# Token order of q, k, v and alpha in a fused gated linear attention and MLP kernel

## The chip, the cores and the metric

The kernel runs on one core of one Trainium2 chip. The metric is the device time of one launch in microseconds, lower is better; a kernel's time is the median of several executions. A separate execution is recorded by the hardware profiler; its span is counted from the first to the last instruction.

The names in the profile: PE is TensorE's matmuls and PEld its weight loads, DVE is VectorE, ACT ScalarE, POOL GpSimd, SP SyncE. SyncE issues nearly all transfers, in program order. A name with a q (SPq) is an engine's instruction queue.

## What is computed

Four batches, eight heads, 768 tokens, head width 48. A recurrent attention with a per-token, per-channel gate `alpha` gives `y`, which is joined over heads to rows of 384 and goes through a layer norm, two matrix products and a residual:

```python
for t in range(S):
    state = alpha[:, :, t, :, None] * state + np.einsum('bhd,bhe->bhde', k[:, :, t], v[:, :, t])
    y[:, :, t] = np.einsum('bhd,bhde->bhe', q[:, :, t], state)
...
xn = (x - mu) / np.sqrt(var + 1e-06) * g_ln
ch = np.maximum(xn @ w_ch1, 0.0) @ w_ch2
return (x + ch)
```

The weights `w_ch1` (384 x 1536) and `w_ch2` (1536 x 384) are double precision; everything else is 32 bits. In memory q, k, v and alpha lie as batch, token, head, width, so one token of one batch is a row of 384 numbers, 1,536 bytes.

## The kernel before

**Tiling.** The tokens are cut into six chunks of 128, one token per partition. `attention(c, b)` (lines 280 to 463) does chunk `c` of batch `b`: ln of alpha (L289), a prefix sum over tokens as a matmul with a triangle, exp of it (L299, L300), scaling of k and q (L302, L304), transposes (L320), scores, masking (L346, L351), the state update `ups` (L367, L376 to L382), the output `yps` (L392, L408), the layer norm and a transposed, scaled copy `xT` (L453, L456, L460) for the MLP. Chunk 0 is done whole (`whole`); in chunks 1 to 5 the 128 tokens are two halves of 64, so that every matmul of the attention covers one quarter, 64 by 64, of the array, and matmuls on different quarters run side by side.

**Pairs of batches.** For chunks 1 to 5 the prefix sums (`sums()`, L471) and the scores (`scores()`, L487) are done for an even and an odd batch together, so that the two use different quarters. In `sums()` the even batch's sum of partition half `h` is written to half `1 - h`: its two halves come out exchanged against alpha's. To match, q, k and v of even batches are loaded with the two halves exchanged: tokens 64 to 127 on partitions 0 to 63. In `attention`, `odd` is 1 for even batches of chunks 1 to 5 (and 0 for odd batches and chunk 0); where the order of tokens counts, the half is `s ^ odd`: state update, gate, and state in the output product. The output rows come out exchanged, and `send` puts them right.

**The second copy of v.** For tokens of half `s` the output product needs v on the partitions on which the scores lie, which is the other half for some heads. `vx`, a second load of half of v's columns with halves placed otherwise, serves these (L163, L164).

**Loads.** `loads("a")`, `loads("k")`, `loads("q")` and `loads_of_v()` yield after each step. Chunk 0 is loaded batch by batch; chunks 1 and 2 two batches at a time (384 KB); chunks 3 to 5 again batch by batch, the odd one first. A load in natural order is one issue (L139, v: L157). A load with the even batch exchanged is a pair of issues, one per partition half, with addresses from `of_pair` (L143, v: L155). `of_pair` gives for half `h` of the partitions the rows of two batches: with `cols` absent, the even batch's half `1 - h` and the odd batch's half `h`.

**Order.** Each unit of work is a generator, and the string `ORDER` names which one takes its next step; every engine runs its instructions in the order in which they were emitted. `0`, `1`, `2` and `3` are the loads of alpha, k, q and v, `4` the sums, `5` the scores, small letters `attention`, `A` to `L` the weight pieces (`take_weights`: load at L207, then the rounding from double to single precision at L219 to L229, in three staging buffers), `Y` and `Z` the first MLP product of chunk 0 (L514), `M` and `V` the later MLP (L626, L803). SyncE's queue also carries, in that order, the gate's way through memory (`row`, L309, then `gate`, L357), the attention's rows (`kept`, L430; read back as `ob`, L497) and the outputs (`send`, L502, L505).

Of the kernel before, what the change touches and what calls it, by code (L numbers as in the profile page):

```python
# [48 lines left out]
def kernel(  # L49
# [36 lines left out]
    nc = tc.nc  # L86

    B, S, H, D = q.shape
    DM = H * D
    DF = w_ch1.shape[1]  # L90
    P = 128
    NCB = S // P
    NP = H // 2
    R = 64 + D
# [15 lines left out]
    HS = P // 2  # L110
    halves = [slice(HS * s, HS * s + HS) for s in range(2)]
    raws = {}

    def of_pair(src, c, m, h, cols=None):

        a = src[2 * m:2 * m + 2, c * P:(c + 1) * P].rearrange("b t h d -> b t (h d)")
        (sb, _), (st, _), _ = a.ap
        if cols is None:
            first, step, n = (1 - h) * HS * st, sb + (2 * h - 1) * HS * st, DM
        else:  # L120
            first, step, n = h * (HS * st + cols), sb + (1 - 2 * h) * (HS * st + cols), cols
        return bass.AP(a.tensor, a.offset + first, [[st, HS], [step, 2], [1, n]])

    def loads(n):

        src = {"a": alpha, "k": k, "q": q}[n]
        lone = None
        for c in range(NCB):
            for m in range(B // 2):
                if c < 3:  # L130
                    t = raw.tile([P, 2, 2, NP, D], FP32, name=f"r{n}", tag="in", bufs=6)
                elif lone is None:
                    t = lone = raw.tile([P, 2, 2, NP, D], FP32, name=f"r{n}", tag="in", bufs=6)
                step = 2 if 0 < c < 3 else 1
                for i in ((0, 1) if c == 0 else (0,) if step == 2 else (1, 0)):
                    bs = slice(2 * m + i, 2 * m + i + step)
                    to = t[:, i:i + step].rearrange("t b i p d -> t b (i p d)")
                    if n == "a" or c == 0 or (step == 1 and i == 1):
                        nc.sync.dma_start(  # L139
                            to, src[bs, c * P:(c + 1) * P].rearrange("b t h d -> t b (h d)"))  # L140
                    else:
                        for h in range(2):
                            nc.sync.dma_start(to[halves[h]], of_pair(src, c, m, h)[:, i:i + step])  # L143
                    raws.update({(n, c, 2 * m + j): t[:, j] for j in range(i, i + step)})
                    yield

    def loads_of_v():
        for c in range(NCB):
            for m in range(B // 2):
                bs, rows = slice(2 * m, 2 * m + 2), slice(c * P, (c + 1) * P)  # L150
                vn = raw.tile([P, 2, 2, NP, D], FP32, name="vn", tag="vn")
                to = vn.rearrange("t b i p d -> t b (i p d)")
                if c:
                    for h in range(2):
                        nc.sync.dma_start(to[halves[h]], of_pair(v, c, m, h))  # L155
                else:
                    nc.sync.dma_start(to, v[bs, rows].rearrange("b t h d -> t b (h d)"))  # L157
                raws.update({("v", c, 2 * m + i): vn[:, i] for i in range(2)})
                yield
                if c:  # L160

                    vx = raw.tile([P, 2, NP, D], FP32, name="vx", tag="vx")
                    for h in range(2):  # L163
                        nc.sync.dma_start(vx[halves[h]].rearrange("t b p d -> t b (p d)"),  # L164
                                          of_pair(v, c, m, h, NP * D))
                    raws.update({("x", c, 2 * m + i): vx[:, i] for i in range(2)})
                    yield
# [100 lines left out]
    def qk_of(c, b):  # L268
        return qks[b if c == 0 else b ^ 1 if c == 1 else (b ^ 1) % 3]
# [10 lines left out]
    def attention(c, b):  # L280


        whole, last = c == 0, c + 1 == NCB
        odd = 0 if whole else 1 - b % 2
# [23 lines left out]
        gate = work.tile([P, 2, NP], FP32, name="gate", tag="gate", bufs=B)  # L308
# [7 lines left out]
        qT = work.tile([R, NP, 2, HS], FP32, name="qT", tag="sum", bufs=11)  # L316
# [14 lines left out]
        if whole:  # L331
            aps = [ps.tile([P, NP, 2, HS], FP32, name=f"aps{i}", tag="bank", bufs=8)
                   for i in range(2)]
            for p in range(NP):
                for i in range(2):
                    rs = slice(64 * i, 64 * i + D)
# [7 lines left out]
        if whole:  # L344
            for i in range(2):
                nc.vector.copy_predicated(  # L346
                    out=at[:, :, i].rearrange("k p s t -> k p (s t)"),
                    data=aps[i].rearrange("k p s t -> k p (s t)"),
                    mask=mask.unsqueeze(1).broadcast_to([P, NP, P]))
        else:  # L350
            nc.vector.copy_predicated(  # L351
                out=at.rearrange("k p s t -> k (p s) t"),
# [10 lines left out]
        for p in range(NP):  # L363
            for s, up in enumerate(ups):
                for i, h in enumerate(heads):
                    ts = slice(0, P) if whole else halves[s ^ odd]
                    nc.tensor.matmul(up[h, p], qk_of(c, b)[ts, 1, p, i, :h.stop - h.start],  # L367
                                     vn[ts, i, p], start=True, stop=True)
        yield

        now, nxt = sts[b][(c + 1) % 2], sts[b][c % 2]
        mid = None if whole else work.tile([R, NP, D], FP32, name="mid", tag="mid", bufs=3)
        for s, up in enumerate(ups):
            by = gate[:R, s ^ odd].unsqueeze(2).broadcast_to([R, NP, D])
            if whole:
                nc.vector.tensor_mul(nxt, up, by)  # L376
                yield
                continue
            old, new = ((now, mid), (mid, nxt))[s]
            nc.vector.tensor_add(new, up, old)  # L380
            yield
            nc.gpsimd.tensor_mul(new, new, by)  # L382
            yield
# [5 lines left out]
        for p in range(NP):  # L389
            for i in range(2 if whole else 0):  # L390
                for s in range(2):
                    nc.tensor.matmul(yps[0][halves[s], i, p], at[:, p, i, s], vn[:, i, p],  # L392
                                     start=True, stop=True)
            for n in range(0 if whole else 8):

                if odd:
                    inner, s, i = n // 4, n // 2 % 2, n % 2
                    r = i
                else:
                    i, s, r = n // 4, n // 2 % 2, n % 2  # L400
                    inner = r != i
                if inner:
                    of, by = at[halves[r], p, s], (vn[halves[r], i, p] if s == r else
                                                   raws["x", c, b][halves[r], p])
                else:
                    rs = slice(64 * i, 64 * i + D)
                    of, by = qT[rs, p, s], (now, mid)[s ^ odd][rs, p]
                nc.tensor.matmul(yps[r][halves[s], i, p], of, by, start=not (odd and inner),  # L408
                                 stop=bool(inner or not odd), skip_group_check=bool(odd))
        yield  # L410
# [87 lines left out]
                yield  # L498

    def send(c, b, cols=slice(0, DM)):  # L500
        if c == 0 or b % 2:
            nc.sync.dma_start(out[b, c * P:(c + 1) * P, cols], ob_of[c, b][:, cols])  # L502
            return
        for h in range(2):
            nc.sync.dma_start(out[b, c * P + HS * (1 - h):][:HS, cols], ob_of[c, b][halves[h], cols])  # L505

    def hidden(h, j):

# [11 lines left out]
    ops_of, ob_of = {}, {}  # L520

    def project(c, b, js):
        if js[0] == 0:
            ops_of[b] = ps.tile([P, DM], FP32, name="ops", tag="bank", bufs=8)
        for j in js:
            nc.tensor.matmul(ops_of[b], hT_of[c][:, j, b], w2[:, j],  # L526
                             start=(j == 0), stop=(j == NJ - 1))
        yield
        if js[-1] == NJ - 1:
            nc.vector.tensor_add(ob_of[c, b], ops_of.pop(b), ob_of[c, b])  # L530
            send(c, b)
            yield
# [86 lines left out]
    def product(c, n):  # L619
# [47 lines left out]
        elif n == 6:  # L667
            sub(o(1))
            late(o(1), e)
            late(o(1), f)  # L670
            send(c, 0)
        elif n == 14:
            copy(out=g, in_=acc)
# [203 lines left out]

    turns = {"YZ"[h]: first_of_chunk_0(h) for h in range(2)}
    turns |= {"012"[i]: loads("akq"[i]) for i in range(3)} | {"3": loads_of_v()}
    turns |= {"PQ"[h]: second_of_chunk_0(h) for h in range(2)}  # L880
    turns |= {"4": sums(), "5": scores()}
    turns |= {chr(ord("a") + n): attention(n // B, n % B) for n in range(NCB * B)}
    turns |= {chr(ord("A") + i): take_weights(i) for i in range(len(pieces))}
    turns |= {"M": mlp(), "V": hidden_products(NCB - 1), "S": combine_first(), "W": combine_weights(), "R": relus(),
# [34 lines left out]
```

## Time and profile before

| what | value |
|---|---|
| median of 3 runs | 434.1 us (433.73 to 434.27) |
| profiled execution, its own time | 432.86 us |
| its span | 431.0 us |
| TensorE clock granted | 1.000 |
| DMA, mean over the span | 105 GB/s, 45.36 MB |

The time of an execution is a little more than its span. In the views that follow, a row of the chain is start, length, what; a row of a timeline is start, duration, engine, line, operation, written tile <- read tiles, count, and in brackets the idle time ahead of it with what ended it. That releaser is inferred: where the engine named had long been done, it was something else, often a transfer. Rows of stretches give the busy time of each engine with the count of its instructions, the granted clock, the mean busy share of the 16 DMA engines and the bytes moved.

### The profile page before, as it was taken

What the parts mean: (1) busy time and instruction counts of PE and PEld (TensorE: products, weight loads), DVE (VectorE), ACT (ScalarE), POOL (GpSimd) and SP (SyncE); (2) the same over time, 40 slices, a digit from 0 to 9 for tenths busy, and PEclk for the clock granted to TensorE, in tenths of its full rate; (3) what the DMA queues carried; (4) which work ended last, traced back from release to release, by engine and by line L of the source; (5) the groups of instructions that cost most, each with busy time, mean ns of one, the idle gap of its engine ahead of it and who ended that gap; (6) DMA issues with size and microseconds to landing.
All of it is one profiled execution on the core that took longest, in us unless ns stands there. A gap on an engine that the chain in (4) does not pass through costs nothing.

```text
span 431.0 us, 11712 instructions
## 1 busy us (share of the span) xinstructions
PE 420.9 (98%) x4760; PEld 373.1 (87%) x4760; DVE 331.2 (77%) x634; ACT 205.9 (48%) x539; POOL 152.2 (35%) x171
## 2 busy tenths in 40 slices
PE   7998999999999999999999999999999999999996
PEld 6887888856778889998889988898998899999996
DVE  4997999899997978886758768657595669675972
ACT  6684556662762567723773353663518442311200
POOL 3020103010027381236652243671154551637313
PEclk9999999999999999999999999999999999999999
DMA  7789788796363343323314034301014000002201
GB/s 256 199 233 256 221 203 186 226 281 177 101 184 107 93 132 84 104 59 91 86 53 123 20 102 104 74 2 40 2 57 128 2 0 3 0 20 63 66 18 55
DMA packets 52717, 45.36 MB, mean 105 GB/s; under 512 B 24076, under 2 KB 48780, under 8 KB 52664
## 3 DMA queue, kind: packets, MB, share of 16 engines
q1 hardware_dynamic: 52264, 44.62, 37.6%
q8 instruction: 37, 0.61, 0.6%
q14 instruction: 16, 0.13, 0.1%
q10 hardware_dynamic: 400, 0.00, 0.1%
HBM read 35.08 MB, written 9.53 MB: 103 GB/s over the span
## 4 chain that ended last, share of the span: by engine, by line
PE 89%; DMA 5%; DVE 2%; ACT 1%; SPq 1%; issue 1%; DVEq 0%
PE ops L626 30%; PE hps L803 30%; PE ops L526 7%; PE hps L514 6%; PE yps L408 4%; PE tps L320 3%; PE aps L487 2%; DMA ra<-in_alpha_dram 2%; PE ups L367 2%; PE xps L453 2%; DMA ws<-in_moe_w_ch_dram 2%; DMA vn<-in_v_dram 1%; PE lps L471 1%; DVE w L221 0%; DVE ws L227 0%
## 5 line engine op out<-in xcount | busy, mean ns | idle before, releaser
L642 POOL TENSOR_TENSOR ob<-ob,u 128x192 f32<-128x192 f32 x40 | 26.6, 676 | 70.5 <-DVE ob L639 53.2
L803 PE MATMUL hps<-sum,w 128*128 128x256 f32 x192 | 47.7, 380 | 0.0
L382 POOL TENSOR_TENSOR mid<-mid,gate 112x192 f32<-112x192 f32 x20 | 13.5, 679 | 87.9 <-DVE mid L380 48.0
L626 PE MATMUL ops<-w,hT 128*128 128x192 f32 x224 | 40.5, 327 | 0.0
L803 PEld LDWEIGHTS hps<-sum,w 128*128 128x128 f32 x192 | 35.8, 190 | 4.6
L626 PEld LDWEIGHTS ops<-w,hT 128*128 128x128 f32 x224 | 37.0, 190 | 0.5
L854 ACT ACTIVATE hT<-hT 128x512 f32<-128x512 f32 x48 | 28.2, 630 | 16.1 <-POOL hT L825 6.7
L803 PE MATMUL hps<-xT,w 128*128 128x256 f32 x136 | 35.1, 382 | 0.0
L514 PE MATMUL hps<-xT,w 128*128 128x256 f32 x144 | 33.0, 383 | 1.4 <-DVE w L229 1.4
L526 PE MATMUL ops<-w,hT 128*128 128x384 f32 x96 | 32.0, 488 | 0.0
L514 PEld LDWEIGHTS hps<-xT,w 128*128 128x128 f32 x144 | 26.6, 190 | 5.2 <-issue 1.5
L626 PE MATMUL ops<-ws,sum 128*128 128x192 f32 x160 | 28.6, 327 | 0.0
L803 PEld LDWEIGHTS hps<-xT,w 128*128 128x128 f32 x136 | 25.3, 190 | 3.3 <-DVE hT L835 0.2
L526 PEld LDWEIGHTS ops<-w,hT 128*128 128x128 f32 x96 | 17.7, 190 | 11.6 <-DVE w L229 0.4
L626 PEld LDWEIGHTS ops<-ws,sum 128*128 128x128 f32 x160 | 26.1, 190 | 0.1
L636 DVE TENSOR_TENSOR ob<-ops,ob 128x192 f32<-128x192 f32 x50 | 17.0, 352 | 10.9 <-PE ops L626 5.7
L327 ACT COPY qT<-tps 112x512 f32<-112x512 f32 x24 | 13.9, 584 | 23.1 <-PE tps L320 23.0
L626 PE MATMUL ops<-ws,hT 128*128 128x192 f32 x128 | 23.9, 328 | 0.9 <-issue 0.9
L320 PE MATMUL tps<-consts,qk 128*112 128x128 f32 x176 | 23.3, 274 | 0.5 <-DVE qk L304 0.5
L822 POOL TENSOR_TENSOR hT<-hT,u 128x512 f32<-128x512 f32 x8 | 10.8, 1356 | 33.7 <-DVE u L821 33.7
L320 PEld LDWEIGHTS tps<-consts,qk 128*112 128x112 f32 x176 | 19.9, 134 | 3.2 <-issue 1.1
L626 PEld LDWEIGHTS ops<-ws,hT 128*128 128x128 f32 x128 | 21.1, 190 | 1.4 <-issue 1.2
(240 smaller groups left out, 1129.1 us busy)
## 6 DMA issues: line engine op xcount, KB each, us to landing
ws<-in_moe_w_ch_dram SPq DMA_DIRECT2D x12, 768.0 KB
kept<-x SPq DMA_DIRECT2D x24, 192.0 KB
ob<-kept SPq DMA_DIRECT2D x24, 192.0 KB
vn<-in_v_dram SPq DMA_DIRECT2D x20, 192.0 KB
rq<-in_q_dram SPq DMA_DIRECT2D x18, 192.0 KB
rk<-in_k_dram SPq DMA_DIRECT2D x18, 192.0 KB
ra<-in_alpha_dram SPq DMA_DIRECT2D x16, 192.0 KB
out_dram<-ob SPq DMA_DIRECT2D x30, 96.0 KB
```

What stands on the lines that cost most here:

```text
L320: nc.tensor.transpose(tps[:, p], qk_of(c, b)[:, i, p].rearrange("p a b -> p (a b)")[:, :R], ident)
L327: nc.scalar.copy(out=qT, in_=tv)
L382: nc.gpsimd.tensor_mul(new, new, by)
L408: nc.tensor.matmul(yps[r][halves[s], i, p], of, by, start=not (odd and inner), stop=bool(inner or not odd), skip_group_check=bool(odd))
L514: nc.tensor.matmul(hps, w1[:, j // 2, f, j % 2 * P:][:, :P], xT_of[0][:, f, bs], start=(f == 0), stop=(f == NF - 1))
L526: nc.tensor.matmul(ops_of[b], hT_of[c][:, j, b], w2[:, j], start=(j == 0), stop=(j == NJ - 1))
L626: nc.tensor.matmul(acc, lhs[:, j], rhs[:, j], start=(j == 0), stop=(j == NT - 1))
L636: nc.vector.tensor_add(x, acc, x)
L642: getattr(nc.gpsimd, f"tensor_{op}")(x, x, y)
L803: nc.tensor.matmul(acc[:, i], w, b, start=True, stop=True)
L822: add_late(c4, c4, u2)
L854: nc.scalar.activation(out=x, in_=x, func=AFT.Relu)
```

## The change

q, k and v are loaded in natural token order everywhere. Even batches of chunks 1 to 5 have alpha loaded with the halves exchanged instead, so that the sums, which exchange them again, come out in natural order. `odd` no longer enters the choice of halves; the second copy of v gets other addresses to match; the outputs of even batches leave in one issue. `ORDER`, `sums()` and `scores()` stay as they are, and so does every matmul's shape and count.

```diff
         (sb, _), (st, _), _ = a.ap
+        first = (1 - h) * HS * st
         if cols is None:
-            first, step, n = (1 - h) * HS * st, sb + (2 * h - 1) * HS * st, DM
+            step, n = sb + (2 * h - 1) * HS * st, DM
         else:
-            first, step, n = h * (HS * st + cols), sb + (1 - 2 * h) * (HS * st + cols), cols
+            first, step, n = first + h * cols, sb + (1 - 2 * h) * cols, cols
...
-                    if n == "a" or c == 0 or (step == 1 and i == 1):
+                    if n != "a" or c == 0 or (step == 1 and i == 1):
                         nc.sync.dma_start(
                             to, src[bs, c * P:(c + 1) * P].rearrange("b t h d -> t b (h d)"))
                     else:
...
-                if c:
-                    for h in range(2):
-                        nc.sync.dma_start(to[halves[h]], of_pair(v, c, m, h))
-                else:
-                    nc.sync.dma_start(to, v[bs, rows].rearrange("b t h d -> t b (h d)"))
+                nc.sync.dma_start(to, v[bs, rows].rearrange("b t h d -> t b (h d)"))
...
-                    ts = slice(0, P) if whole else halves[s ^ odd]
+                    ts = slice(0, P) if whole else halves[s]
...
-            by = gate[:R, s ^ odd].unsqueeze(2).broadcast_to([R, NP, D])
+            by = gate[:R, s].unsqueeze(2).broadcast_to([R, NP, D])
...
-                    of, by = qT[rs, p, s], (now, mid)[s ^ odd][rs, p]
+                    of, by = qT[rs, p, s], (now, mid)[s][rs, p]
...
     def send(c, b, cols=slice(0, DM)):
-        if c == 0 or b % 2:
-            nc.sync.dma_start(out[b, c * P:(c + 1) * P, cols], ob_of[c, b][:, cols])
-            return
-        for h in range(2):
-            nc.sync.dma_start(out[b, c * P + HS * (1 - h):][:HS, cols], ob_of[c, b][halves[h], cols])
+        nc.sync.dma_start(out[b, c * P:(c + 1) * P, cols], ob_of[c, b][:, cols])
```

In numbers of issues: k and q each lose 10 (one for each of the four two-batch loads of chunks 1 and 2, one for each of the six loads of an even batch in chunks 3 to 5), v loses 10, the outputs lose 10, alpha gains 10.

## The prediction

> **What bounds the kernel now.** I read the page first, then the chain of waits in order of time, the waits of TensorE, and last the issues of the SyncE queue. From the page:
>
> ```profile
> span 431.0 us, 11712 instructions
> PE 420.9 (98%) x4760; PEld 373.1 (87%) x4760; DVE 331.2 (77%) x634; ACT 205.9 (48%) x539; POOL 152.2 (35%) x171
> PE   7998999999999999999999999999999999999996
> PE 89%; DMA 5%; DVE 2%; ACT 1%; SPq 1%; issue 1%; DVEq 0%
> ```
>
> TensorE is busy for 98% of the span and is 89% of the chain. The DMA share of the chain, 5%, must then sit where the row of slices has its 7 and 8: at the start. The chain in order of time (start, length, what) says where:
>
> ```profile
> 8.22 6.39 DMA vn<-in_v_dram
> 14.62 1.73 DMA gate<-row
> 16.35 4.23 DMA ra<-in_alpha_dram
> 20.61 0.52 ACT la L289
> ...
> 29.03 0.61 SPq L143
> ...
> 30.35 6.85 DMA ws<-in_moe_w_ch_dram
> 37.22 0.58 DVE w L219
> ...
> 41.71 0.97 DVE w L229
> 42.81 9.31 PE hps L514 x42
> ...
> 427.43 0.36 DVE ob L636
> ```
>
> Until 42.81 us the chain is loads and what they release: v of chunk 0, alpha of chunk 1, then the second weight piece (ws at 30.35, called B here), which VectorE rounds from 37.22 to 42.68. From 42.81 on it is TensorE to the end. The change removes no matmul, so it can gain by bringing the 42.81 forward, and in the last microseconds after TensorE. TensorE's waits after 30 us:
>
> ```profile
> PE hps L514 <- DVE w L229: 1.4, 1, 1.4
> ```
>
> TensorE had finished what comes before at 42.81 - 1.4 = 41.4 and stood for B.
>
> **Whole loads against halved ones.** Before, a two-batch load of v, k or q behind chunk 0 is a pair of issues, each into 64 partitions. Busy time by stretch (TensorE, weight loads, VectorE, ScalarE, GpSimd, clock, DMA share, GB/s):
>
> ```profile
> 7.00:11.00 4.00, 3.53 (x22) 2.43 (x22) 2.83 (x6) 3.51 (x9) 0.00 (x0) 1.00 1.07 372
> 69.00:71.00 2.00, 2.00 (x108) 1.74 (x107) 1.93 (x3) 1.01 (x3) 1.86 (x2) 1.00 1.07 229
> 43.00:97.00 54.00, 53.98 (x728) 42.51 (x727) 50.68 (x84) 33.11 (x80) 7.01 (x11) 1.00 0.83 223
> ```
>
> In the first stretch whole loads are under way, in the second halved ones; the DMA engines are full in both. 384 KB are 393,216 bytes: 1.06 us at 372 GB/s, 1.72 us at 229. So a load made whole saves **0.66 us** of transfer, and one cut in two (alpha) costs as much.
>
> The row stands first; the Trainium skill, SBUF — State Buffer, section "Door 1: The DMA port swizzle", says that 64 partitions reach 8 of the 16 DMA ports, measures 196 GB/s there against 328 at 1 MiB, and says that two transfers to the two halves do not add up. By those figures an estimate is 0.8 us for each such load in place of the row's value; alpha, now the only one cut, would pay 0.3 us more over its two early loads, which speaks for the slower rival below.
>
> Issues of the SyncE queue (start, duration):
>
> ```profile
> 8.22 0.43 SPq L157 DMA_DIRECT2D vn<-in_v_dram  x1
> 8.75 0.26 SPq L309 DMA_DIRECT2D row<-eq  x1
> 9.06 0.33 SPq L139 DMA_DIRECT2D rq<-in_q_dram  x1
> 9.44 1.43 SPq L143 DMA_DIRECT2D rk<-in_k_dram  x2
> 10.98 0.37 SPq L309 DMA_DIRECT2D row<-more  x1
> 11.40 0.34 SPq L357 DMA_DIRECT2D gate<-row  x1
> 12.61 0.22 SPq L309 DMA_DIRECT2D row<-more  x1
> ...
> 14.99 1.26 SPq L143 DMA_DIRECT2D rq<-in_q_dram  x2
> 16.35 1.30 SPq L139 DMA_DIRECT2D ra<-in_alpha_dram  x1
> ...
> 24.20 1.90 SPq L155 DMA_DIRECT2D vn<-in_v_dram  x2
> 26.14 1.25 SPq L143 DMA_DIRECT2D rk<-in_k_dram  x2
> ...
> 28.50 0.35 SPq L430 DMA_DIRECT2D kept<-x  x1
> 28.94 1.35 SPq L143 DMA_DIRECT2D rq<-in_q_dram  x2
> ```
>
> A whole 384 KB load is issued in 0.43 us, a pair in 1.25 to 1.90. Ahead of B five pairs become singles: 7.19 us of issuing become about 5 x 0.45 = 2.25, and 5 x 0.66 = 3.3 us of transfer go. Two alpha loads (chunk 1) become pairs: +0.8 us of issuing and +0.66 us of transfer each.
>
> **What of this is on the path, step by step.**
>
> Step 1, B's issue. SyncE waits at 28.50 for x (kept). Behind it stands only the q pair, then B. 1.35 becomes 0.45: B goes out at 29.45 in place of 30.35, **-0.9**.
>
> Step 2, B's flight, 6.85 us in a line behind v, k and q. Only q shorter: -0.66; all three: -2.0. B lands at 29.45 + 4.9 to 6.2 = 34.3 to 35.6, not at 37.20.
>
> Step 3, VectorE must be free for it. Its rows (and the wait in brackets), with TensorE's weight load of the same time:
>
> ```profile
> 29.12 0.66 PEld L367 LDWEIGHTS ups<-vn,qk 64*64 64x64 f32 x32 [0.71 <-DVE ws L227]
> 33.73 0.56 DVE L304 TENSOR_TENSOR qk<-rq,more 128x384 f32<-128x384 f32 x1 [0.65 <-DMA rq<-in_q_dram]
> 35.07 1.01 DVE L456 TENSOR_TENSOR xT<-xps,small 128x384 f32<-128x384 f32 x2
> ```
>
> It is done with L456 at 36.08, after 0.65 us of standing for q. q is issued 0.9 us shorter and moved 0.66 us faster, so that wait goes: free at 35.43. The later of steps 2 and 3 is about 35.5, so rounding starts **1.7** us earlier and B is ready at 41.0.
>
> Step 4, TensorE must be there by then. The 0.71 us before L367 is put down to L227, which writes ws and nothing that this matmul reads; I take v's pair (24.20, 1.90 us) for the late one. Whole, it is issued 1.4 us shorter: the stall goes, and TensorE arrives at 41.4 - 0.7 = 40.7. L514 then starts near 41.1, **-1.7**. If only step 1 counts it is -0.9; if VectorE's work ahead of L456 moves too, -2.4.
>
> Step 5, alpha of chunk 1, which was on the chain. The gate load at 14.62 reads no v, yet v's landing releases it: it is the eighth issue behind v (8.75, 9.06, two at 9.44, 10.98, 11.40, 12.61, 14.62), so I read that eight are in flight at most. With k a single, the eighth is q: the gate goes near 12.9, q at about 14.65. q takes 0.45, alpha's halves 0.63 each (half of 1.25) or, at worst, 1.30 each: done at 16.4 to 17.7, against 17.65. Adding the 2.93 us that it lands after its issue, and 0.66: 20.0 to 21.3, against 20.58. v's own landing is pushed 0.66 by the first alpha pair, which stands ahead of it, and relieved as much by k behind it, whose halves shared the engines with it. I take 0 for this step, with -0.6 to +0.7.
>
> Step 6, what becomes of the gain later. VectorE is busy for 50.68 of 54 us from 43 to 97, but its chain starts with B, so it moves along. Alpha has no room at one place, chunk 3 (issues; ln; the chain's row of the sums):
>
> ```profile
> 75.81 0.86 SPq L139 DMA_DIRECT2D ra<-in_alpha_dram  x2
> ...
> L289 ACT ACTIVATE la<-ra x2: 526/527/528, 79.9 to 80.7; 128x384 f32<-128x384 f32 x2
> ...
> 81.23 0.90 PE lps L471 x6
> ```
>
> The second ln ends as the sums start, and with them everything behind on TensorE. The even batch's load becomes two issues (+0.6) and moves slower (192 KB: 0.53 to 0.86, +0.33). The queue ahead is lighter, so I hand back **+0.4**, between 0 and 0.9.
>
> Step 7, the tail:
>
> ```profile
> 426.52 1.11 SPq L505 DMA_DIRECT2D out_dram<-ob  x2
> 427.72 1.02 SPq L502 DMA_DIRECT2D out_dram<-ob  x2
> ```
>
> The second issue at L502 starts near 428.3, behind the pair and its neighbour, though its add ended at 427.43 + 0.36 = 427.79. With one issue fewer ahead it goes at once: **-0.45**.
>
> Costed at nothing: the other 8 output pairs (TensorE's matmuls cover them), and the row order of the even batches' update matmuls, which no row of before shows apart. A matmul there takes about 0.22 us:
>
> ```profile
> L367 PE MATMUL ups<-vn,qk x112: 199/218/253, 14.7 to 30.8; 64*64 64x48 f32 x32, 64*48 64x48 f32 x32, 128*64 128x48 f32 x24, 128*48 128x48 f32 x24
> ```
>
> One fill more or less at each border of the 10 even updates is at most ±2.2 us; inside an update the tiles still alternate, so I take 0.
>
> Sum: -1.7 + 0.4 - 0.45 = -1.75 us. The profiled execution took 432.86 with its span of 431.0; the median is 1.24 above it, and I carry the difference over: 434.1 - 1.75 = 432.3. Its own range is 431.2 (-2.4, nothing handed back) to 433.3 (step 1 and the tail alone, 0.55 of it lost).
>
> **Rivals.**
>
> *Everything moves.* v of chunk 0 lands about 1 us earlier, since k behind it is whole; then alpha, VectorE and TensorE all gain that microsecond, and nothing is handed back: -1.75 - 1.0 - 0.4, **430.9**. For it: v takes 6.39 us, far over 1.06. Against: the alpha pair ahead of it.
>
> *The gain is eaten.* VectorE's 94% from 43 to 97 or a load leaves TensorE waiting until the 1.7 are gone; only the tail is left: **433.6**. Against: TensorE waits nowhere there now.
>
> *Slower: cut alpha becomes the late load.* Place: ln of chunk 1's second pair, at 20.61. v at +0.66 holds q to 15.3; with 0.45 for q and 1.30 for alpha's first half the second goes out at 17.05. If the line before it is as full as v's was (6.39 us from issue to landing), it lands at 23.4; I take 22.9, ln late by 2.3. VectorE's room is 37.22 - 35.43 = 1.8, so it decides from an ln at 22.4. At +2.3 VectorE is done with L456 at 36.08 + 2.3 - 0.65 = 37.7, B is ready 0.5 late, and chunk 3 adds 0.9 with no room: 0.5 + 0.9 - 0.45 = +0.95, **435.1**. Against: q and k give back issue time right ahead of it.
>
> *It does not do what it says.* The words name other column tiles for the scores, but the scores are not in the diff and no matmul is added or dropped; this case has the times above and no chance of its own.
>
> **How the numbers follow.** Forecast 0.55, everything moves 0.13, eaten 0.18, slower 0.14. What can be told from no change is 0.2%, 0.87 us. Faster: 0.55 + 0.13 = 0.68; same: 0.18; slower: 0.14. The range runs from 430.6, below "everything moves", to 434.6, which leaves out most of the slower case and holds the eaten one and much of the update matmuls' bound.
>
> **What would show it.** Right: L514's first wait for L229 under 0.6 us and its start near 41.1; B issued before 29.6 and landed by 35.7; no stall before the first L367 of chunk 1; the gate near 12.9; one issue at L502 following 427.79 at once. Step 5 is wrong if ln (20.61) starts after 21.3; step 6 if the sums of chunk 3 follow their ln later than TensorE could run them, or by more than 0.9 us. The forecast is wrong if L514 starts after 42, or if TensorE shows new waits of over 1 us between 43 and 427.

## The result, and the profile after

| comparison (the kernel before on the same chip) | before, median | changed, median | ratio and its 95% interval |
|---|---|---|---|
| first, 7 and 7 runs | 433.69 us | 430.42 us | 0.9933 [0.9911, 0.9956] |
| again, 23 and 12 runs | 432.35 us | 430.50 us | 0.9963 [0.9936, 0.9990] |

The change is faster, by 3.3 us in the first comparison and 1.9 us in the second; 432.3 us and -1.75 us had been forecast. The direction held. The range of 430.6 to 434.6 had been written for a kernel before at 434.1 us, and a ratio of 0.9933 makes 431.2 of that, inside the range; 430.42 itself, beside a kernel before of 433.69, lies 0.2 us below it. Where the granted clock of each run is on record, the 77 of 93 runs of the kernel before with 0.998 or more have a median of 432.4 us and the 18 of 19 such runs of the changed kernel 430.4, a difference of 2.0 us; runs with a lower clock took longer. Most terms of the sum did not hold, and most of this part is about that. The page of the changed kernel, first profile:

```profile
span 428.4 us, 11650 instructions
PE 420.9 (98%) x4760; PEld 372.9 (87%) x4760; DVE 330.7 (77%) x634; ACT 205.9 (48%) x539; POOL 153.2 (36%) x171
PE 87%; DMA 6%; DVE 3%; ACT 1%; issue 1%; SPq 0%; POOL 0%; DVEq 0%; ACTq 0%
```

Engine work is what it was; the 62 instructions fewer are semaphores and DMA issues. The chain of waits of the changed kernel (start, length, what):

```profile
14.85 5.75 DMA ra<-in_alpha_dram
...
20.68 0.52 ACT la L286
...
29.52 7.14 DMA ws<-in_moe_w_ch_dram
...
36.68 0.57 DVE w L216
...
41.09 0.97 DVE w L226
...
42.20 9.31 PE hps L507 x42
...
79.38 6.25 DMA ws<-in_moe_w_ch_dram
...
87.80 0.66 DVE at L348
...
88.50 8.01 PE ops L519 x24
...
425.60 0.36 DVE ob L629
```

It is the old chain with new line numbers: alpha, then B, then TensorE. L507 (L514 before) starts at 42.20, not near 41.1, although B was issued at 29.52 as foreseen. The SyncE queue (start, duration, issue) shows what alpha did:

```profile
13.29 0.32 SPq L354 DMA_DIRECT2D gate<-row  x1
13.75 0.40 SPq L140 DMA_DIRECT2D rq<-in_q_dram  x1
14.20 1.25 SPq L144 DMA_DIRECT2D ra<-in_alpha_dram  x2
```

In these first profiles alpha of chunk 1 went out 2 us earlier than before (14.20 against 16.35), and its ln started at the same time (20.68 against 20.61). In the second ones, h1 and h2 below, it went out at the same time (14.84 against 14.73), and its ln started 1.5 us later (20.90 against 19.43). Two profiles of each kernel, cut at the start on B and at the last add of the output, say where the time went:

| us | before, 1st | before, 2nd | changed, 1st | changed, 2nd | difference of the means |
|---|---|---|---|---|---|
| first layer on B starts | 42.81 | 42.60 | 42.20 | 42.97 | -0.12 |
| from there to the start of the last add | 384.62 | 383.80 | 383.40 | 382.90 | -1.06 |
| from there to the end of the span | 3.57 | 3.60 | 2.80 | 2.83 | -0.77 |
| span | 431.0 | 430.0 | 428.4 | 428.7 | -1.95 |

So the start, on which the forecast had put -1.7, gave about nothing. The tail gave 0.77. The middle, for which +0.4 was forecast, gave 1.06. Three more traces below have the same loads as one of the two kernels: e1 and h3 as the changed one, h4 as the kernel before. With them the start gives -0.5 us (42.48 in the mean of four, 42.96 in the mean of three) and the middle -0.7; each start spreads over 0.8 to 0.9 us within one kernel.

### The profile page after: what moved, and what is told of

It reads as the page before. It is cut to its first block, busy times and chain, and to the rows that moved or that the text cites. A ratio compares the mean times of both kernels' runs of the same rounds, so it can differ in the third digit from the quotient of the medians.

```text
span 428.4 us, 11650 instructions
## 1 busy us (share of the span) xinstructions
PE 420.9 (98%) x4760; PEld 372.9 (87%) x4760; DVE 330.7 (77%) x634; ACT 205.9 (48%) x539; POOL 153.2 (36%) x171
## 4 chain that ended last, share of the span: by engine, by line
PE 87%; DMA 6%; DVE 3%; ACT 1%; issue 1%; SPq 0%; POOL 0%; DVEq 0%; ACTq 0%
PE ops L619 31%; PE hps L796 30%; PE hps L507 6%; PE ops L519 6%; PE yps L405 4%; DMA ws<-in_moe_w_ch_dram 3%; PE tps L317 3%; DMA ra<-in_alpha_dram 2%; PE ups L364 2%; PE aps L484 2%; PE xps L450 2%; PE lps L468 1%; DMA rq<-in_q_dram 1%; DVE w L218 1%; DVE at L343 1%
## 5 line engine op out<-in xcount | busy, mean ns | idle before, releaser
L619 PE MATMUL ops<-w,hT 128*128 128x192 f32 x224 | 40.7, 327 | 0.1
L847 ACT ACTIVATE hT<-hT 128x512 f32<-128x512 f32 x48 | 28.2, 630 | 16.4 <-POOL hT L818 7.0
L507 PE MATMUL hps<-xT,w 128*128 128x256 f32 x144 | 33.0, 383 | 0.6 <-DVE w L226 0.6
L519 PE MATMUL ops<-w,hT 128*128 128x384 f32 x96 | 32.3, 489 | 0.3 <-DVE at L348 0.3
L507 PEld LDWEIGHTS hps<-xT,w 128*128 128x128 f32 x144 | 26.6, 190 | 4.4 <-issue 0.7
L619 PE MATMUL ops<-ws,sum 128*128 128x192 f32 x160 | 28.6, 327 | 0.0
L519 PEld LDWEIGHTS ops<-w,hT 128*128 128x128 f32 x96 | 17.7, 190 | 12.2 <-DVE at L348 0.9
L619 PE MATMUL ops<-more,sum 128*128 128x192 f32 x120 | 22.0, 326 | 0.0
## 6 DMA issues: line engine op xcount, KB each, us to landing
vn<-in_v_dram SPq DMA_DIRECT2D x12, 384.0 KB, 4.7
```

Source lines behind the costliest of these rows:

```text
L507: nc.tensor.matmul(hps, w1[:, j // 2, f, j % 2 * P:][:, :P], xT_of[0][:, f, bs], start=(f == 0), stop=(f == NF - 1))
L519: nc.tensor.matmul(ops_of[b], hT_of[c][:, j, b], w2[:, j], start=(j == 0), stop=(j == NJ - 1))
L619: nc.tensor.matmul(acc, lhs[:, j], rhs[:, j], start=(j == 0), stop=(j == NT - 1))
L847: nc.scalar.activation(out=x, in_=x, func=AFT.Relu)
```

## The experiments

All kernels but h1, h2 and h4 are the changed kernel with one edit; their medians stand against its 430.45 (the 19 runs of both comparisons).

**Undoing one part at a time.** Three kernels put back one of the halved parts each, and a fourth leaves alpha whole.

e1: the outputs of even batches leave in two issues again.

```diff
-        nc.sync.dma_start(out[b, c * P:(c + 1) * P, cols], ob_of[c, b][:, cols])
+        if c == 0 or b % 2:
+            nc.sync.dma_start(out[b, c * P:(c + 1) * P, cols], ob_of[c, b][:, cols])
+            return
+        for h in range(2):
+            nc.sync.dma_start(out[b, c * P + HS * h:][:HS, cols], ob_of[c, b][halves[h], cols])
```

> The changed kernel, with the outputs of even batches of chunks 1 to 5 sent in two issues again, as before the change. Theory A (the time hangs on when the chain of loads lets TensorE start the first MLP product, L507 at 42.20 us in the changed kernel, and on the last issues after TensorE): only the tail comes back, +0.45 us, a time of about 430.9 and a ratio to the kernel before of 0.9943; L507 stays at 42.2. Theory B (the time follows the number of halved transfers): 10 pairs more, each hidden by matmuls, but half as fast; no place of its own, +0 to +0.5.

e2: v of chunks 1 to 5 in two halves, in natural order.

```diff
-                nc.sync.dma_start(to, v[bs, rows].rearrange("b t h d -> t b (h d)"))
+                vr = v[bs, rows].rearrange("b t h d -> t b (h d)")
+                for h in halves if c else [slice(0, P)]:
+                    nc.sync.dma_start(to[h], vr[h])
```

> The changed kernel, with v of chunks 1 to 5 loaded in natural order but in two issues of 64 partitions each. Theory A: v lands later (about 29 us in place of 27.8) but TensorE waits for a bank until 30.02 anyway, so +0 to +0.3 us, about 430.5, ratio 0.994. Theory B: ten loads at +0.66 us of transfer each, those of chunk 1 and 2 seen: +1 us or more, 431.4 or above.

e3: the same for k and q.

```diff
-                        nc.sync.dma_start(
-                            to, src[bs, c * P:(c + 1) * P].rearrange("b t h d -> t b (h d)"))
+                        rows = src[bs, c * P:(c + 1) * P].rearrange("b t h d -> t b (h d)")
+                        cut = n != "a" and c and not (step == 1 and i == 1)
+                        for h in halves if cut else [slice(0, P)]:
+                            nc.sync.dma_start(to[h], rows[h])
```

> The changed kernel, with k and q of chunks 1 to 5 loaded in natural order but in two issues where the kernel before had two. Theory A: the second weight piece is issued behind one q pair, 0.9 us later (30.4 in place of 29.52), and moves in a longer line; L507 starts at 42.8 to 43.2 in place of 42.20 and the time is +0.6 to +1.0 us, about 431.2, ratio 0.996. Theory B: like v's pairs, +1 us or more.

e4: alpha whole and not exchanged. The exchange is left out, so the gates of even batches belong to the other half of the tokens.

```diff
-                    if n != "a" or c == 0 or (step == 1 and i == 1):
+                    if True:
```

> The changed kernel, with alpha loaded whole, in one issue. It then leaves out the exchange of halves for even batches, so their gates belong to the other half's tokens. Theory A1 (alpha's halves are what delays it): alpha of chunk 1 lands about 1 us before its 20.6, L286 of the second pair starts by 19.7, L507 by 41.3, time -0.9 us, about 429.5, ratio 0.991. Theory A2 (one of the 16 DMA engines is late by 1 to 2 us because a 16 KB piece of program code comes through it at that moment, and holds back alpha and later the weight piece): alpha lands at 20 or later all the same, L507 stays within 0.4 us of 42.2, ratio 0.9925 to 0.994.

| kernel | median, us | ratio to before | first layer on B | last add to end |
|---|---|---|---|---|
| e1, outputs cut | 430.63 | 0.9943 [0.9922, 0.9965] | 42.56 | 3.54 |
| e2, v cut | 431.38 | 0.9968 [0.9946, 0.9990] | 43.17 | 2.90 |
| e3, k and q cut | 433.16 | 1.0005 [0.9982, 1.0028] | 44.03 | 3.05 |
| e4, alpha whole | 428.67 | 0.9906 [0.9886, 0.9927] | 40.49 | 2.96 |

e1 gives back the tail: 3.54 us behind the last add, as before the change. Its median, 0.2 us up, is too near to show the 0.7. e2 and e3 show that the part on the loads was no illusion: whole v is worth 0.9 us of the median (0.3 to 1.7 when the runs are resampled, 95%), whole k and q 2.7 (1.2 to 3.6). Four of e3's twelve runs had a granted clock of 0.996 and took 433.2 us or more; the other eight have a median of 432.3, 1.9 up. e4 shows who takes it back: alpha, cut in halves, costs 1.8 us (1.3 to 2.5). At the start the signs are the same: against the changed kernel's mean of 42.59, cut v is +0.6, cut k and q +1.4, whole alpha -2.1. These are single traces, and 0.6 is within the spread of one kernel; but what v, k and q bring there, 2.0, is about what alpha eats.

**Which alpha.** g1 loads alpha of chunk 1 alone whole, and takes its sums unexchanged; nothing is left out.

```diff
-                    if n != "a" or c == 0 or (step == 1 and i == 1):
+                    if n != "a" or c < 2 or (step == 1 and i == 1):
...
-                        nc.tensor.matmul(lps[halves[h ^ i ^ 1], :DM], tri[halves[h], halves[h]],
+                        nc.tensor.matmul(lps[halves[h if c == 1 else h ^ i ^ 1], :DM], tri[halves[h], halves[h]],
```

> The changed kernel, but chunk 1 has alpha whole and in natural order, and its sums write the natural half for both batches (two matmuls on the same quarter instead of four quarters at once). If halved alpha of chunk 1 alone is what the change pays at the start: ln of the second pair at 18.2 as with alpha whole everywhere, L507 at 40.5 to 41.0 (0.3 us at most for the slower sums), and the time 1.2 to 1.7 us under the changed kernel, about 428.9, ratio 0.990. If halved alpha in chunks 2 to 5 is what cost there: L507 stays near 42.2 and the time near 430.3.

428.61 us, 0.9900 [0.9857, 0.9942]: all of e4's gain, from two loads of one chunk. It beats both kernels. Its chain, where B leaves at 28.64:

```profile
28.64 6.28 DMA ws<-in_moe_w_ch_dram
...
34.94 0.57 DVE w L216
...
39.15 0.97 DVE w L226
...
40.25 5.85 PE hps L507 x26
```

The issue of alpha and its ln (ScalarE, with its wait in brackets), first in the changed kernel, then in g1:

```profile
14.20 1.25 SPq L144 DMA_DIRECT2D ra<-in_alpha_dram  x2
20.68 0.52 ACT L286 ACTIVATE la<-ra 128x384 f32<-128x384 f32 x1 [2.04 <-DMA ra<-in_alpha_dram]
```

```profile
13.76 1.33 SPq L140 DMA_DIRECT2D ra<-in_alpha_dram  x1
19.39 0.52 ACT L286 ACTIVATE la<-ra 128x384 f32<-128x384 f32 x1 [0.17 <-DMA ra<-in_alpha_dram]
```

Whole, alpha is there 1.3 us sooner: it is issued 0.4 us earlier and is 0.8 us less on its way (which of the two counts was not separated further). ScalarE stands 0.17 us for it in place of 2.04, and x, the wait ahead of B in the queue, follows: 27.28 in place of 28.56. Not all that comes behind is alpha's: B is issued 0.9 us earlier and lands 1.7 us earlier, since its last share is less late in this execution (the table under steps 2 and 3).

**B earlier by itself.** g3 moves q and B in `ORDER` ahead of SyncE's wait for x.

```diff
-    "bbfabbceeddeeeafffbbhdcccfA3bAa1dddAddccc5fdd24gB3eeeCAfefghhccceYhcgYYddhhccgYh"
+    "bbfabbceeddeeeafffbbhdcccfA3bAa12BdddAddccc5fdd4g3eeeCAfefghhccceYhcgYYddhhccgYh"
```

> The changed kernel, but q of chunk 1's second pair and the second weight piece are issued right behind k, ahead of the rows (kept) for which SyncE stands from 25.2 to 28.56. If L507 hangs on the landing of the weight piece (36.66): it lands near 32.5, VectorE takes it when it is free, near 35, and L507 starts at 40.6 to 41.3; time 0.9 to 1.6 us under the changed kernel, about 429.1, ratio 0.990. If L507 hangs on alpha and what follows it on VectorE and TensorE: L507 at 41.8 to 42.2, time 430.0 to 430.4.

430.62 us, 0.9951 [0.9926, 0.9976]: a miss. B was issued at 26.11 and TensorE no longer waited for it, yet the 42 matmuls on B came at 44.67. Three rows say why, two of TensorE's waits after 28 us and a stretch (busy time of the engines, then granted clock, DMA share, GB/s):

```profile
PE ups L364 <- issue: 1.0, 1, 1.0
PE ups L364 <- ACT x L418: 0.7, 1, 0.7
```

```profile
34.00:38.00 4.00, 4.00 (x15) 3.25 (x14) 1.40 (x4) 0.63 (x3) 0.51 (x1) 0.61 0.97 324
```

In this execution the clock granted to TensorE was 0.61 for 4 us, worth 1.6 us, and 1.0 us is a wait of the kind treated below. Without both it would be 42.1: what TensorE has to do before B was itself due near 41.6 (42.20 - 0.6 and 42.97 - 1.3 in the changed kernel), so by this B alone can bring no more than its wait of 0.6 to 1.3 us. Why the clock fell was not tried; six of the twelve runs of g3 had 0.995 or 0.996.

**Pieces of TensorE's program among the loads.** A transfer of 16 KB, which belongs to no line of the kernel, shows in the views of the DMA queues; the changed kernel has one between 16 and 18 us:

```profile
q1 hardware_dynamic: 389, 0.54, 98.4%
q8 instruction: 1, 0.02, 3.0%
```

There are 37 in a run, and TensorE's 9,598 instructions are 37.5 times 256. An issue that meets one often takes longer: in the 14 traces, 76 of the 171 issues of q, k, v, alpha and weights that overlap such a transfer took over 0.9 us, and 8 of the 1,154 others. In the second profile of the changed kernel a piece starts at 29.0:

```profile
29.24 1.15 SPq L140 DMA_DIRECT2D rq<-in_q_dram  x1
30.44 0.51 SPq L204 DMA_DIRECT2D ws<-in_moe_w_ch_dram  x1
```

The single q took 1.15 us, not 0.46, and B left at 30.44, where the pair of before had let it go at 30.35. f1 and f2 shift these pieces with fewer or more warming matmuls, which compute nothing that is used.

```diff
-    for _ in range(8):
-        nc.tensor.matmul(idle[:, :P], zero, zero, start=True, stop=True)
+    for i in range(4 + 32):
+        wide = P if i < 4 else 8
+        nc.tensor.matmul(idle[:wide, :wide], zero[:, :wide], zero[:, :wide], start=True, stop=True)
```

That is f2; f1 has `range(1)` in place of `range(8)`.

> The changed kernel with 1 warming matmul at the start in place of 8, 28 TensorE instructions fewer, so that the 16 KB pieces of program code, one for 256 instructions, come some 0.7 us later against the loads (near 17.3 in place of 16.6). Theory F (code pieces hold up alpha: SyncE's issue takes 1 us more while one is under way, and the DMA engine that carries it lands its sixteenth late): alpha of chunk 1 is issued and mostly moved before it, ln of the second pair starts at 19.5 to 20.0 in place of 20.68, L507 0.5 to 1.0 us before 42.20, time about 429.7. Theory H (alpha's half rate alone): ln at 20.4 to 20.8, L507 at 42.0 to 42.6, time 430.3.

> The changed kernel with 4 warming matmuls and 32 tiny ones, 112 TensorE instructions more, so that the code pieces come some 2.5 us earlier against the loads (near 14.1, then near 20). Theory F: the piece meets the issue of q and alpha themselves, alpha is issued up to 1 us later and lands at 20.4 to 21.4; L507 at 42.2 to 43.2, time 430.3 to 431.3. Theory H: ln at 20.4 to 20.8, L507 at 42.0 to 42.6, time 430.3.

f1: 431.27 us, 0.9963 [0.9933, 0.9993]. The first piece did not come later (15.9 us; 16.6 and 14.8 in the two profiles of the changed kernel), so its premise failed; the others came at 25.7 and 29.2, the last met the issue of q, B left at 30.96, and L507 started at 43.22. f2: 434.18 us, 1.0028 [0.9994, 1.0062], with pieces at 13.8, 19.7 and 29.4, ln at 21.80 and the first layer on B at 42.93. L507 is where its theory had it, ln is later than it had it, and most of the time was lost elsewhere, in two waits of TensorE; eight of its ten runs also had a granted clock of 0.992 to 0.996. The start of the first piece differs by 1.8 us between two executions of one kernel, so f1 and f2 do not decide between F and H. The two waits:

```profile
PE aps L485 <- issue: 2.0, 1, 2.0
...
PE yps L406 <- issue: 1.2, 1, 1.2
```

**The middle.** TensorE of the kernel before stood twice for nothing visible. h1 and h2 are the two kernels unedited, for second profiles.

> The changed kernel once more, for a second profile and more times. What is open: of the 2.6 us between the two profiled spans, 0.9 to 1.0 is a stretch in which TensorE of the kernel before waited for nothing that the profile shows (0.93 us at 292.9, before L626). Theory L (it belongs to that one execution): this profile starts the first layer on B (L507, x42) at 42.0 to 42.4 again, since that comes from the loads, while gaps of the kind 'issue' of 0.4 to 1.5 us may stand anywhere or nowhere; median 430.1 to 430.8, ratio 0.993 to 0.9965. Theory K (the changed kernel is free of such gaps): none over 0.3 us after 43 us here either.

> The kernel before once more, as a kernel of the comparison, for a second profile. Theory L: the first layer on B (L514) starts at 42.6 to 43.1 again, and the last add of the output follows 384.0 to 385.5 us later; the gap of 0.93 us at 292.9 is gone, or has another size or place; its total of gaps of the kind 'issue' on TensorE after 43 us differs from the first profile's 1.4 us by over 0.3. Theory K: 0.9 to 1.0 us before L626 near 292.9 again. Time: ratio 0.997 to 1.003 to itself under both.

TensorE's waits in h2, the second profile of the kernel before, after 30 us:

```profile
PE hps L514 <- DVE w L229: 1.6, 1, 1.6
PE ups L367 <- ACT x L421: 0.7, 1, 0.7
PE ups L367 <- issue: 0.3, 1, 0.3
PE ops L626 <- issue: 0.3, 1, 0.3
```

h1 (430.50 us) started on B at 42.97, outside L's 42.0 to 42.4, and had no wait over 0.3 us after 43 us, as K had it. h2 (431.93 us, 0.9995 [0.9974, 1.0017]) had 0.66 us of such waits, another size as L had it, but at K's two places; its last add followed after 383.80 us, just under L's 384.0. So the places belong to the kernel and the sizes to the execution. At the second place, near 293, all three traces of the kernel before wait (h4 below is the third), and none of the eight with the changed kernel's number of TensorE instructions does; at the first, near 257, two of those eight (e4 and g1) wait 0.2 us or more as well. TensorE's timeline there, the kernel before (first and second profile, wait in brackets), then the changed kernel:

```profile
292.51 0.43 PE L626 MATMUL ops<-ws,hT 128*128 128x192 f32 x1
293.87 0.92 PE L626 MATMUL ops<-ws,hT 128*128 128x192 f32 x4 [0.93 <-issue]
```

```profile
292.09 0.43 PE L626 MATMUL ops<-ws,hT 128*128 128x192 f32 x1
292.85 1.41 PE L626 MATMUL ops<-ws,hT 128*128 128x192 f32 x7 [0.33 <-issue]
```

```profile
290.83 1.09 PE L364 MATMUL ups<-vn,qk 64*64 64x48 f32 x32
291.85 1.57 PE L619 MATMUL ops<-ws,hT 128*128 128x192 f32 x8
```

h3 and h4 tested whether a piece of VectorE's program, which came in at 292 in the kernel before and at 300 in the changed one, is the cause: memsets on VectorE, idle at that time, shift it.

```diff
+    for _ in range(18):
+        nc.vector.memset(least, -8.0 * (896 << 20))
```

h3 is this on the changed kernel, h4 with 16 on the kernel before.

> The changed kernel with 18 more memsets of a small tile on VectorE at the start, where it is idle (2.7 to 7.4 us); nothing else is moved. VectorE's program is fetched in pieces of 8 KB; one of them goes at 300.5 to 300.7 in both profiles of the changed kernel, at 292.1 to 292.5 in both of the kernel before, whose TensorE waited 0.3 to 0.9 us for nothing visible at 292.5 to 292.9. The 18 memsets put the changed kernel's piece at 291.5 to 292.0, beside the same TensorE work. Theory Q (that piece delays TensorE's own program): a gap of 0.3 to 1.0 us before the first L619 after L364 at 292 to 293, median 0.3 to 1.0 above the changed kernel's (430.7 to 431.5). Theory R (the gap has nothing to do with it): no gap over 0.2 us between 288 and 296, median 430.2 to 430.7, ratio 0.994 to 0.997.

> The kernel before with 16 such memsets at the same place: its piece of VectorE's program moves from 292.1 to 292.5 to some 284. Theory Q: the gap of 0.3 to 0.9 us at 292.5 to 292.9 is gone, the one at 257.4 to 257.7 (beside a piece of ScalarE's program, which stays) is still there at 0.3 to 0.5; ratio 0.997 to 0.9995. Theory R: both gaps are there; ratio 0.999 to 1.001.

h3: 430.25 us, 0.9939 [0.9917, 0.9960], no such wait; but the piece only moved to 295.5, so this says little. h4: 431.94 us, 0.9984 [0.9960, 1.0008]; its piece left 292 for 290.2, and both waits stayed, 0.2 us in the middle of the same update and 0.65 after the same first matmul:

```profile
292.73 0.43 PE L628 MATMUL ops<-ws,hT 128*128 128x192 f32 x1
293.81 1.08 PE L628 MATMUL ops<-ws,hT 128*128 128x192 f32 x5 [0.65 <-issue]
```

VectorE's piece is not it. Counting TensorE's instructions (weight loads, matmuls, semaphores) up to each wait of this kind of 0.2 us or more after 30 us gives:

```
profile               wait, us      instructions ahead    remainder by 256
before, 1st           0.48, 0.93    7106, 7872            194, 192
before, 2nd           0.33, 0.33    7104, 7874            192, 194
h4 (before)           0.21, 0.65    7104, 7873            192, 193
changed, 2nd (h1)     0.34          960                   192
g3                    1.00          960                   192
e4; g1                0.38; 0.20    7104                  192
f2                    2.05, 1.21    2752, 7872            192, 192
```

All stand at one place of a piece of 256, to within two. The 1.30 us of f2 at 31.67, which the profile puts down to ScalarE, and 0.36 us of h3 at 28.34 stand at that place too (960 and 704 ahead). The transfers say the same. With borders and 16 KB transfers counted in order, TensorE goes on 1.25 to 1.55 us after the transfer's packet has ended in all fourteen of these waits, and at none of the other 491 borders in the 14 traces does it pass sooner than 1.25 us after. So TensorE waits there for its next piece; where no wait is seen at a border, the piece came in time. The Trainium skill, Runtime: NRT & Kernel Launch, section "Instruction fetch mechanics", says that the program comes in blocks of 16 KiB, 256 instructions, over a DMA queue of the engine's own, at a cost that is "mostly hidden". The blocks agree with the 37 pieces here; hidden it was not at these borders, with up to 2.05 us.

## Why the prediction was right and wrong

*The rates held.* Where the v, k and q that are issued near 65 us move, the halves of before went at 229 GB/s (69 to 71 us), the whole loads of the changed kernel at 346 (68 to 70).

*Step 1 held, once.* B was issued at 29.52, foreseen 29.45. In the second profile the q load met a piece of the program and took 0.7 us more, and B left at 30.44. The step also took x as fixed at 28.50. In the four traces with the changed loads x goes out at 28.6, 28.8, 29.3 and 29.9 and B at 29.5 to 30.8; with the loads of before x goes at 28.1 to 28.6 and B at 30.3 to 30.4; with alpha whole (g1, e4) x goes at 27.3 and 26.9. So x comes later in the changed kernel, and earlier again once alpha is whole.

*Steps 2 and 3 failed at the landing.* B was to be 4.9 to 6.2 us on its way and to land by 35.6; it took 7.14 and 6.95 us in the two profiles, no less than before (6.85 and 6.64). The trace marks the landing of a transfer in 16 shares. In the first profile 15 of B's were there in time, the last was not, and q ahead of it went the same way:

```
transfer                          issued   15 of 16 landed   last
changed, alpha, second half       14.85    19.7              20.6
changed, q ahead of B             29.00    32.6              33.9
changed, B                        29.52    34.8              36.7
changed, 2nd (h1), B              30.44    36.0              37.4
before, B                         30.35    36.5              37.2
g1, B                             28.64    34.5              34.9
```

In the four rows of the changed kernel the last share comes 0.9 to 1.8 us behind the others. That this has to do with the piece at 28.1 or 34.2 was not shown. Step 3 had VectorE's wait for q gone and VectorE free at 35.43. The wait stayed in the first profile (a row of VectorE's waits), and VectorE was done with L453 at 36.26:

```profile
DVE qk L301 <- DMA rq<-in_q_dram: 0.8, 1, 0.8
```

*Step 4 failed.* The 0.71 us before L367 was put down to v's pair, and rightly: its second half landed at 29.02, and the weight load went at 29.12. Whole, v landed at 27.79 and the weight load went at 28.66. But the stall did not leave the path: TensorE now stands at the next instructions of the same update, for an evacuation by ScalarE, and goes on at 30.02, against 29.97 before. TensorE's weight load there, before and changed, then its waits in the changed kernel:

```profile
29.97 0.19 PEld L367 LDWEIGHTS ups<-vn,qk 64*64 64x64 f32 x4 [0.18 <-ACT x L421]
30.02 0.19 PEld L364 LDWEIGHTS ups<-vn,qk 64*64 64x64 f32 x4 [0.54 <-ACT x L418]
```

```profile
PE hps L507 <- DVE w L226: 0.6, 1, 0.6
PE ups L364 <- ACT x L418: 0.4, 1, 0.4
PE ops L519 <- DVE at L348: 0.3, 1, 0.3
```

TensorE reached B's matmuls at 41.6, not 40.7.

*Step 5 failed, and with it the -1.7.* "I take 0 for this step": its first half was right. Eight issues in flight did hold the queue, on eight semaphores for landings that are used in turn: before, the gate left at 14.62, 0.01 us after v, eight issues ahead of it, had landed; in the changed kernel the eighth is q, which left at 13.75, after v's 13.68. The value for alpha was wrong. Its halves were issued by 15.45, sooner than the 16.4 to 17.7 foreseen, and still landed at 20.6, no earlier than before: behind its issue it was given 2.93 + 0.66 = 3.6 us and took 5.1 (4.1 in the second profile). ln started 0.07 us later in the first profiles and 1.47 us later in the second, 0.8 in the mean (0.6 with the three more traces), about the bound of +0.7. And that bound was set against the alpha of one execution of the kernel before, which was issued late behind q's pair. The right one is a whole alpha at the new place: ln at 19.39 in g1. e4 and g1 measure the halves at 1.8 us of the median and 2.1 to 2.3 us of the start. The slower rival named this mechanism, and had its place right. The Trainium skill, SBUF — State Buffer, section "Door 1: The DMA port swizzle", quoted in the prediction, pointed the same way: by it alpha would pay 0.3 us more than the row's value. The 1.8 us here are far more; chunk 1's alpha is on the chain, in two loads one behind the other.

*Step 6 was about right.* The sums followed their alpha at chunk 3, and the wait is elsewhere: L519 behind L348, which is queued on VectorE behind the next weight piece (79.38 in the chain). It is 0.3 us in the first profile, not there in the second, 0.5 in g1, 0.7 in f1 and 0.9 in h3; +0.4 had been taken.

*Step 7 held and was too small.* The last issue follows its add at once (the row is three issues in a line; the add ends at 425.96):

```profile
424.69 1.63 SPq L498 DMA_DIRECT2D out_dram<-ob  x3
```

-0.77 in the place of -0.45: the step counted the wait in the queue alone, which is 0.5. The rest is that the span ends 2.45 us after the last issue starts, in place of 2.70; why was not tried.

*What no step had.* The middle's -1.06 is nearly all waits for the program: 1.41 and 0.66 us after 43 us in the two profiles of the kernel before, 1.04 in the mean, and none of 0.2 us there in the two of the changed kernel. With fewer transfers to wait for, TensorE's program lost semaphore instructions (92 to 78), so the same borders of 256 fall on later work: at 292 the border of the kernel before is one matmul behind 64-wide updates of some 30 ns each, that of the changed kernel seven matmuls later (293.09), when the piece is there. That the waits are at the borders is shown; that these 14 instructions alone moved them was not tried.

The forecast of -1.75 came near the -1.95 of the profiles by luck: the start was 1.6 us worse than its step, the middle 1.5 us better, the tail 0.3 us better. Of the 3.3 us of the first comparison, some 1 to 1.4 us are beyond what the second one and the profiles show, and stay open: the kernel before has medians from 432.35 to 433.69 in the comparisons of this study, and the clocks of its runs in the first are not on record.

## What to carry to other kernels

When a fix moves a cost from some transfers to another, price the one that pays at its new place against the same transfer unburdened, not against its old time: here three tensors gained what the fourth, on the chain, took back, and keeping that one whole for a single chunk was worth as much as the change. Where TensorE waits for nothing visible, count its instructions up to the wait: where the counts agree modulo 256 across profiles, as here, it is the program that is late. Which instructions stand at such a border, near a run of small matmuls, was worth 1.4 us in one execution of the kernel before and 3.3 us in f2. For an effect of under 1%, take two profiles of each kernel before a difference is explained: two of the same kernel differed by 0.8 us in the start.

## What the runs showed of the hardware beside this

A piece of TensorE's program can hold up the kernel's own loads in the SyncE issue: one whole 384 KB load is issued in 0.40 to 0.47 us in most places, and took 1.15 to 1.38 us in some where a piece was under way (q at 29.24 in h1 and at 29.53 in f1). It does not always: k at 24.77 in e1 took 0.40 us with a piece under way. Whole loads of 384 KB were issued faster than two halves (0.46 against 1.25 us). And the clock granted to TensorE can fall for a few microseconds: 0.61 from 34 to 38 us in g3, whose mean over the span was 0.995.
